# Softmax attention and an MLP on one core: units 3 to 5 take the 128-key form, with k and v loaded by SyncE

## The chip, the cores and the metric

The kernel runs on one core of a Trainium2 chip. The metric is the device time of one execution in microseconds; it is given as the median of several runs. One of the executions was recorded by the hardware profiler; its page and trace are what is read here. The core's engines are named PE (TensorE, with PEld for its weight loads), DVE (VectorE), ACT (ScalarE), POOL (GpSimd) and SP (SyncE, which here only issues DMAs).

## What is computed

q, k and v are fp32 arrays of 8 batches, 12 heads, 448 positions and 64 dimensions. Attention is computed for each head; the heads of a batch are laid side by side, which gives x with 3584 rows and 768 columns; an MLP with 2048 hidden columns follows.

```python
scores = scale * np.matmul(q, k.transpose(0, 1, 3, 2))      # scale = 1 / sqrt(64)
attn = softmax(scores)
attn_out = np.matmul(attn, v)
x = attn_out.transpose(0, 2, 1, 3).reshape(3584, 768)
h = x @ w_in                                                # 768 x 2048
g = np.maximum(0.01 * h, h)
return g @ w_out                                            # 2048 x 768
```

## The kernel before

Matrix products run on PE in bf16. Attention is tiled in units: unit u is one batch and one pair of heads (u = 6 x batch + pair, `HP` = 6 units a batch, 48 in all). Two heads of 64 dimensions fill PE's 128 rows.

A unit passes through these steps, each a function:

- Load: `load_soft` (L163) issues DMAs on POOL, which convert fp32 to bf16 on the way; `load_one` (L173) issues on SP and leaves fp32. In the first 26 us the buffers for loads are pieces of tensors that are needed only later (`rooms`: pieces of `w_in_mix` first, then of `w_mix`, `o`, `deep_mix`, `c`), each taken once.
- `cast` (L190 to L203) copies the loaded q and k into `qkb` (L190), and v into `v_old` (L198, printed as x_mix in the trace since it lies in that tensor) or `v_sb` (L201 to L203). Units 0 and 1 and the q and k of unit 2, and v of unit 0, are cast by DVE (and ACT for half of unit 0), all others by POOL. The loop `supply(u)` writes out which casts and which DMA issues POOL does in step u, in order.
- `transposes` (L301): eight PE transposes into one PSUM bank, and one copy by DVE to `qkT` (L305).
- `scores(u, c)`: one chunk c of keys against all 448 queries, for both heads; `expo(u, c)`: ACT's exp of that chunk.
- `pv(u, j)`: the exps times v with a column of ones, which gives numerator and denominator; DVE's reciprocal (L374) and multiply (L375) give x.
- `x_transposes` (L389, L390): x turned for the MLP.

There are two forms of chunking. The old form, for units below `HY` = 18, takes the 448 keys in four chunks of `SC` = 112: four pairs of matmuls (L319), four exps over 112 rows and 896 columns (L331 three times, L334 once), and pv by `pairs` (L362), 32 matmuls of 65 columns. The new form, for units from 18 on, takes three chunks of 128 keys (`KC` = 3), and the last 64 keys of both heads share one fourth chunk: one matmul over 128 rows (L322), an exp of 448 columns in place of 896 (L336), and pv by `weighted` (L343, L350): for each of four query chunks one matmul of 130 columns and six of 65. For it k and v lie in another order in the buffers (128 rows: keys 0 to 255 on rows 0 to 63, keys 256 to 447 on rows 64 to 127), so that a cast is a memset (L193), a large copy (L194) and two small ones (L195, L196) for k, and a large copy (L201) and two small ones (L202, L203) for v.

The order of the instructions on every engine is written by hand. It begins with three loads on SP (k of 0, q of 0, k of 1), nine loads of q, k and v on POOL and the first piece of w_in. Then `first(u)` runs for u = 0 to 5: scores and exps of unit u, pv of unit u - 1, the transposes of unit u + 1, x transposes of unit u - 2, and `supply(u)` for POOL. From about 25 us the first batch's MLP products (`part`, L424) are mixed with the attention of later units; from there on the order is the same for both kernels.

w_in comes in three pieces (L215) by POOL's queue, of 4, 6 and 6 blocks of 128 columns, later w_out in four. All POOL loads go through one software queue and land in the order of their issue.

## Time and profile before

| | |
|---|---|
| runs | 377.79, 378.84, 379.81 us, median 378.84 |
| profiled execution | 378.34 us, its span 376.6 us |
| granted PE clock | 0.999 |
| PE busy | 369.7 us, 98% of the span |
| DVE busy | 256.9 us, 68% |
| ACT busy | 259.6 us, 69% |
| POOL busy | 191.8 us, 51% |
| scores of units 1 to 6 start (L319) | 9.49, 12.57, 15.96, 19.09, 22.23, 25.91 us |
| pv of units 1, 2, 3, 4 starts (L362) | 13.58, 16.71, 19.85, 22.98 us |
| w_in's third piece lands | 36.8 us |

How it is read: busy shares are averages over the whole span. The page also cuts the span into 40 slices (of 9.4 us here), with a digit for each engine's busy tenths, the granted PE clock and the DMA engines. The chain of waits goes back from the last instruction to what released each step. A timeline lists groups of instructions of one engine by start; in square brackets stands the idle time before a group and what ended it. "x3" is three instructions in a group. For DMAs the rows give the count, the KB of each, and the median time from issue to landing. POOL's and SP's rows for a DMA are the issue alone.

### The profile page before, as it was taken

To read this page: it belongs to the slowest core of one execution; us is meant where nothing else is said; L and a number is where in the kernel's file an instruction comes from. 1 tells how busy PE (TensorE), PEld (TensorE's weight loads), DVE (VectorE), ACT (ScalarE), POOL (GpSimd) and SP (SyncE) were. 2 spreads that over 40 slices of the span, in tenths; PEclk is the share of its full clock that TensorE was granted. 3 is DMA by queue.
4 is the path that set the end of the run, shared out by engine and by line. 5 is a ranking of instruction groups with operands and counts; after the bars stand their busy time and mean duration, and the time that the engine had idled before them with its cause. 6 is when DMAs were issued, how large, how long until landed. Compare 5 with 4: busy or idle time off the path is not lost.

```text
span 376.6 us, 10120 instructions
## 1 busy us (share of the span) xinstructions
PE 369.7 (98%) x4008; PEld 265.7 (71%) x4008; DVE 256.9 (68%) x558; ACT 259.6 (69%) x399; POOL 191.8 (51%) x376
## 2 busy tenths in 40 slices
PE   7999999999999999999999999999999999999996
PEld 3664658756698556996569966599665995679765
DVE  4765858778666867766676665775847775685763
ACT  5997885866768776758766587666787668636721
POOL 7985871986268989624588235792347020000000
PEclk9999999999999999999999999999999999999999
DMA  9999999999499885973869648798455740321123
GB/s 155 200 203 207 191 204 201 156 159 164 93 178 143 114 163 87 197 158 60 157 121 148 144 64 86 170 147 167 61 66 98 143 110 0 79 58 45 42 65 105
DMA packets 99600, 48.08 MB, mean 128 GB/s; under 512 B 64608, under 2 KB 96352, under 8 KB 99552
## 3 DMA queue, kind: packets, MB, share of 16 engines
q0 software_dynamic: 39600, 22.47, 44.6%
q1 hardware_dynamic: 59504, 24.50, 32.6%
q8 instruction: 31, 0.51, 0.6%
q10 hardware_dynamic: 448, 0.47, 0.4%
q14 instruction: 17, 0.14, 0.1%
HBM read 45.61 MB, written 11.01 MB: 150 GB/s over the span
## 4 chain that ended last, share of the span: by engine, by line
PE 94%; DMA 2%; DVE 1%; issue 1%; POOL 1%; ACT 1%; POOLq 0%; ACTq 0%; DVEq 0%
PE g L682 30%; PE g L548 14%; PE sc L548 14%; PE sc L322 7%; PE sc L350 6%; PE g L424 4%; PE sc L319 4%; PE sc L645 4%; PE sc L362 3%; PE g L817 2%; PE sc L343 2%; DMA w_in_mix<-in_v_dram 2%; PE g L362 1%; PE g L301 1%; PE sc L424 1%
## 5 line engine op out<-in xcount | busy, mean ns | idle before, releaser
L331 ACT ACTIVATE e<-sc 128x896 bf16<-128x896 f32 (+1 forms) x144 | 123.6, 923 | 30.7 <-PE sc L322 20.8
L682 PE MATMUL g<-w_out_sb,h 128*128 128x384 bf16 (+1 forms) x440 | 84.1, 325 | 0.0
L682 PEld LDWEIGHTS <-h 128*128 128x128 bf16 x592 | 54.4, 98 | 41.4 <-issue 11.2
L537 ACT ACTIVATE h<-c 128x512 bf16<-128x512 f32 (+1 forms) x72 | 43.1, 610 | 30.2 <-DVE c L563 12.4
L548 PEld LDWEIGHTS <-w_in_sb 128*128 128x128 bf16 x576 | 54.6, 98 | 5.7
L190 POOL COPY qkb<-fq 112x512 bf16<-112x512 bf16 x34 | 23.9, 703 | 41.6 <-DMA qkT<-qkb 32.5
L548 PEld LDWEIGHTS <-w_in_mix 128*128 128x128 bf16 x432 | 40.5, 98 | 3.7
L201 POOL COPY v<-fv 128x384 bf16<-128x384 bf16 x30 | 18.5, 617 | 43.1 <-PE sc L350 40.7
L687 DVE COPY o<-g 128x384 f32<-128x384 f32 x47 | 26.0, 553 | 13.7 <-PE g L682 13.5
L350 PE MATMUL sc<-v,e 128*128 128x65 bf16 x720 | 33.3, 193 | 0.0
L322 PE MATMUL sc<-qkT 64*128 64x448 bf16 (+1 forms) x210 | 32.8, 352 | 0.0
L350 PEld LDWEIGHTS <-e 128*128 128x128 bf16 x720 | 31.1, 98 | 1.3
L974 DVE RECIPROCAL rec<-sc 112x8 f32<-112x8 f32 x42 | 8.7, 207 | 33.6 <-PE sc L350 19.1
L975 DVE TENSOR_TENSOR x<-sc,rec 112x512 bf16<-112x512 f32 x42 | 29.0, 691 | 1.6 <-DVE rec L974 0.2
L548 PE MATMUL g<-xT,w_in_sb 128*128 128x256 bf16 (+1 forms) x216 | 28.5, 268 | 0.0
L548 PE MATMUL sc<-xT,w_in_sb 128*128 128x256 bf16 (+1 forms) x216 | 28.5, 268 | 0.0
L693 DVE TENSOR_TENSOR o<-o,g 128x384 f32<-128x384 f32 x39 | 21.4, 549 | 9.1 <-PE g L682 4.4
L343 PE MATMUL sc<-v,e 128*128 128x130 bf16 x120 | 26.5, 221 | 0.0
L649 DVE TENSOR_TENSOR o<-o,sc 128x192 f32<-128x192 f32 x39 | 13.7, 351 | 17.9 <-PE sc L645 17.9
L682 PE MATMUL g<-w_mix,h 128*128 128x384 bf16 x128 | 24.6, 326 | 0.2 <-DVE o L687 0.2
L163 POOL DMA_DIRECT2D fv<-in_v_dram x32 | 20.1, 641 | 7.7 <-DMA fq<-in_q_dram 3.1
L682 PE MATMUL g<-w_mix,hmix 128*128 128x384 bf16 x112 | 21.7, 326 | 0.0
(149 smaller groups left out, 744.1 us busy)
## 6 DMA issues: line engine op xcount, KB each, us to landing
fq<-in_q_dram POOLq DMA_DIRECT2D x17, 224.0 KB, 5.7
w_out_sb<-in_moe_w_out_dram POOLq DMA_DIRECT2D x4, 768.0 KB, 13.2
out_dram<-o SPq DMA_DIRECT2D x7, 336.0 KB, 3.4
w_in_sb<-in_moe_w_in_dram POOLq DMA_DIRECT2D x2, 1152.0 KB, 12.7
out_dram<-o SPq DMA_DIRECT2D x7, 288.0 KB, 3.4
fk<-in_k_dram POOLq DMA_DIRECT2D x15, 128.0 KB, 5.9
fv<-in_v_dram POOLq DMA_DIRECT2D x15, 128.0 KB, 4.8
out_dram<-o SPq DMA_DIRECT2D x7, 240.0 KB, 3.1
```

Of the source, the lines that this page charges most:

```text
L163: nc.gpsimd.dma_start(out=t[p, :n, :, :so].rearrange("p u h so d -> p (u h) (so d)"), in_=(q, k, v)[x][b, hs, keys].rearrange("h (p so) d ...
L190: by(t[:SC, x].rearrange("p so h d -> p h so d"), f)
L322: nc.tensor.matmul(ps[:, j, :S].rearrange("p (so s) -> p so s", so=NSC), t[p, 1, c], t[p, 0, :, :SC], start=True, stop=True,)
L331: nc.scalar.activation(e[:, :, c, :], ps[:n, :, :S], AX.Exp, scale=scale)
L343: nc.tensor.matmul(ps, e[:, EM + qc * SC:EM + qc * SC + P], vt[:, 2 * KC:].rearrange("p j d -> p (j d)"), start=True, stop=False, skip_gro ...
L350: nc.tensor.matmul(ps[:, j * (D + 1):(j + 1) * (D + 1)], e[:, at:at + P], vt[:, j * KC + c], start=False, stop=(c == KC - 1), skip_group_c ...
L537: nc.scalar.activation(hs[:, m:m + 2, cols], x.rearrange("p (m t) -> p m t", m=2), AX.Prelu, alpha=0.01)
L548: nc.tensor.matmul(ps[:, j * nh:(j + 1) * nh], w[:, kk, ts(j, P)], x[:, kk], start=(first and j == 0 and kk == 0), stop=(kk == KH - 1), sk ...
L682: nc.tensor.matmul(ps[:, cols], x[:, m], w[:, m], start=(first and m == 0), stop=(m == MH - 1), skip_group_check=True,)
L687: by(o[:, at], ps[:, :NW])
L693: nc.vector.tensor_add(o[:, at], o[:, at], ps[:, :NW])
L975: nc.vector.tensor_mul(x, ps[:, :, :, :D], rec.to_broadcast([SC, 2, 2 * NP, D]))
```

## The change

Units 3, 4 and 5 take the new form. `old(u)` says which units keep the old one: 0 to 2 and 6 to 17. The functions that tested `u < HY` now test `old(u)`, and `pv` calls `weighted` for new units.

k and v of units 3 to 5 are no longer loaded by POOL. A new function `load_into` loads one of them by two SP DMAs, of 64 rows with 2 x 256 and 2 x 192 elements, in fp32, into a buffer whose first content has been cast already: k of 3 into that of q of 1; once v of unit 0 is cast, k of 4, v of 3 and v of 4 into those of v of 0, k of 1 and k of 2; in `supply(0)` k of 5 into that of q of 2 and 3 and v of 5 into that of v of 1 and 2. POOL's casts of them read fp32.

POOL's loads before the first casts are q of 1; q of 2 and 3; k of 2; v of 0; v of 1 and 2; q of 4 and 5; q and k of 6 and 7; then w_in's first piece. The table in `supply` has another order. w_in's pieces have 5, 5 and 6 blocks. Since fewer rooms are needed, three pieces of `w_mix` are no longer among them.

```diff
--- before.py
+++ after.py
@@ -127,14 +127,20 @@
     w_in_v = moe_w_in.rearrange("(ko ki) n -> ki ko n", ki=P)
     w_out_v = moe_w_out.rearrange("(ko ki) n -> ki ko n", ki=P)
 
-    raw = {}
+    FIRST = 3
+
+    def old(u):
+
+        return u < FIRST or HP <= u < HY
+
+    raw, homes = {}, {}
 
 
 
     rooms = []
     for t in (w_in_mix, w_mix):
         t = t.rearrange("p x k n -> p (x k n)")
-        for j in range(9):
+        for j in range(9) if not rooms else range(3, 9):
             rooms.append(t[:, ts(j, 4 * NSC * D)])
     for _ in range(3):
         rooms.append(o_pool.tile([P, DM], F32, name="o").bitcast(BF16)[:, :4 * NSC * D])
@@ -148,18 +154,21 @@
         n = P if x and new else SC
         if not rooms:
             return ld_pool.tile([n, 2, NSC, D], F32, name="f" + "qkv"[x])
-        return rooms.pop(0)[:n].bitcast(F32).rearrange("p (h so d) -> p h so d", h=2, so=NSC)
+        homes["last"] = rooms.pop(0).bitcast(F32).rearrange("p (h so d) -> p h so d", h=2, so=NSC)
+        return homes["last"][:n]
+
+    split = ((slice(0, D), NSC, slice(0, NSC * D)), (slice(D, P), KC, slice(NSC * D, S)))
 
     def load_soft(u, n, which):
         b, hp = divmod(u, HP)
         hs = slice(2 * hp, 2 * hp + 2 * n)
         for x in which:
             new = x > 0 and u >= HY
-            t = room(x, new).rearrange("p h so d -> p (h so d)").bitcast(BF16)
+            t = room(x, new)
+            homes[u, x] = homes["last"]
+            t = t.rearrange("p h so d -> p (h so d)").bitcast(BF16)
             t = t.rearrange("p (u h so d) -> p u h so d", u=2, h=2, so=NSC)
-            for p, so, keys in ((slice(0, D), NSC, slice(0, NSC * D)), (slice(D, P), KC, slice(NSC * D, S))) if new else (
-                (slice(0, SC), NSC, slice(0, S)),
-            ):
+            for p, so, keys in split if new else ((slice(0, SC), NSC, slice(0, S)),):
                 nc.gpsimd.dma_start(
                     out=t[p, :n, :, :so].rearrange("p u h so d -> p (u h) (so d)"),
                     in_=(q, k, v)[x][b, hs, keys].rearrange("h (p so) d -> p h (so d)", so=so),
@@ -170,10 +179,20 @@
     def load_one(u, x, queue):
         b, hp = divmod(u, HP)
         t = room(x, False)
+        homes[u, x] = homes["last"]
         queue.dma_start(
             out=t.rearrange("p h so d -> p h (so d)"),
             in_=(q, k, v)[x][b, 2 * hp:2 * hp + 2].rearrange("h (p so) d -> p h (so d)", so=NSC),
         )
+        raw.setdefault(u, {})[x] = t
+
+    def load_into(u, x, t):
+        b, hp = divmod(u, HP)
+        for p, so, keys in split:
+            nc.sync.dma_start(
+                out=t[p, :, :so].rearrange("p h so d -> p h (so d)"),
+                in_=(q, k, v)[x][b, 2 * hp:2 * hp + 2, keys].rearrange("h (p so) d -> p h (so d)", so=so),
+            )
         raw.setdefault(u, {})[x] = t
 
     def load(u, parts=(0, 1, 2)):
@@ -186,7 +205,7 @@
         for x in parts:
             f = raw[u].pop(x)
             t = qkb[u % NB]
-            if x < 2 and (x == 0 or u < HY):
+            if x < 2 and (x == 0 or old(u)):
                 by(t[:SC, x].rearrange("p so h d -> p h so d"), f)
             elif x == 1:
                 if u < HY + NB:
@@ -194,7 +213,7 @@
                 by(t[:, 1, :KC].rearrange("p so h d -> p h so d"), f[:, :, :KC])
                 by(t[:D, 1, KC, 0], f[:D, 0, KC])
                 by(t[D:, 1, KC, 1], f[:D, 1, KC])
-            elif u < HY:
+            elif old(u):
                 by(v_old[:, u % NV, :, :, :D], f)
             else:
                 t = v_sb[u % NV]
@@ -203,7 +222,7 @@
                 by(t[D:, 2 * KC + 1, :D], f[:D, 1, KC])
 
     w_steps = []
-    for lo, hi in ((0, 4), (4, 10), (10, MD)):
+    for lo, hi in ((0, 5), (5, 10), (10, MD)):
         w_steps.append([t[:, :, lo * P:hi * P] for t in (w_in_sb, w_in_v)])
     for i in range(4):
         w_steps.append([t[:, ts(i // 2 + 2 * (i % 2), MD // 4)] for t in (w_out_sb, w_out_v)])
@@ -220,12 +239,12 @@
     ident = const_pool.tile([P, P], BF16)
     make_identity(nc, ident)
     load_soft(1, 1, (0,))
-    load_soft(2, 2, (0, 1))
+    load_soft(2, 2, (0,))
+    load_soft(2, 1, (1,))
     load_soft(0, 1, (2,))
     load_soft(1, 2, (2,))
-    load_soft(4, 2, (0, 1))
-    load_soft(3, 2, (2,))
-    load_soft(5, 1, (2,))
+    load_soft(4, 2, (0,))
+    load_soft(6, 2, (0, 1))
     load_w(1)
 
     warm = h_mix.rearrange("p m c t -> p (m c t)")[:, :512]
@@ -292,7 +311,7 @@
         return bank.bitcast(BF16)
 
     def transposes(u, bank=None):
-        n = SC if u < HY else P
+        n = SC if old(u) else P
         t, flat = qkb[u % NB], qkT[u % NQ].rearrange("p i c s -> p (i c s)")[:, :2 * NSC * n]
         for parts in ((1,), (0,)) if u == 0 else ((0, 1),):
             tr = turn_tile(bank)[:, :2 * NSC * n].rearrange("p (i s) -> p i s", i=2)
@@ -312,7 +331,7 @@
         ps = next_slot()
         t = qkT[u % NQ]
         sc_t[u, c] = ps
-        if u < HY:
+        if old(u):
             t = t.rearrange("p i c s -> p (i c s)")
             for j in range(2):
                 p = slice(j * D, (j + 1) * D)
@@ -325,11 +344,11 @@
 
     def expo(u, c):
         e, ps = e_sb[u % NE], sc_t.pop((u, c))
-        n = SC if u < HY else P
+        n = SC if old(u) else P
         if c < KC:
             e = e[:n, :EM].rearrange("p (j c s) -> p j c s", j=2, c=KC)
             nc.scalar.activation(e[:, :, c, :], ps[:n, :, :S], AX.Exp, scale=scale)
-        elif u < HY:
+        elif old(u):
             e = e_old[u % NE][:n, :2 * S].rearrange("p (j s) -> p j s", j=2)
             nc.scalar.activation(e, ps[:n, :, :S], AX.Exp, scale=scale)
         else:
@@ -367,14 +386,19 @@
 
         bank = next_bank() if bank is None else bank
         ps = bank[:, :NSC * (D + 1)].rearrange("p (q d) -> p q d", q=NSC)
-        pairs(u, j, ps)
         if j == 0:
             x_t[u] = x_pool.tile([SC, NSC, 2, D], BF16, name="x")
+        if old(u):
+            pairs(u, j, ps)
+            x = x_t[u][:, :, j, :]
+        else:
+            n = 2 * (D + 1)
+            for y in range(NP):
+                weighted(u, j * NP + y, bank[:, y * n:(y + 1) * n])
+            x = x_t[u][:, j * NP:(j + 1) * NP].rearrange("p q j d -> p (q j) d")
         rec = r_pool.tile([SC, NSC, 1], F32, name="rec")
         nc.vector.reciprocal(rec, ps[:SC, :, D:])
-        nc.vector.tensor_mul(
-            x_t[u][:, :, j, :], ps[:SC, :, :D], rec.to_broadcast([SC, NSC, D])
-        )
+        nc.vector.tensor_mul(x, ps[:SC, :, :D], rec.to_broadcast([SC, NSC, D]))
 
     def x_transposes(u, bank=None):
         b, hp = divmod(u, HP)
@@ -850,13 +874,15 @@
 
     def supply(u):
 
-        for what, n, *parts in {0: [('load', 6, (0, 1)), ('qk', 3), ('v', 1), ('v', 2), ('load', 6, (2,))], 1: [('qk', 4), ('v', 3), ('load', 8, (0, 1))], 2: [('qk', 5), ('v', 4), ('w', 1)], 3: [('qk', 6), ('v', 5), ('w', 1)], 4: [('qk', 7), ('v', 6), ('load', 10, (0, 1)), ('load', 8, (2,))], 5: [('qk', 8), ('v', 7), ('load', 10, (2,)), ('load', 12)]}[u]:
+        for what, n, *parts in {0: [('qk', 3), ('v', 1), ('v', 2), ('into', 5, 1, (2, 0)), ('into', 5, 2, (1, 2))], 1: [('qk', 4), ('load', 6, (2,)), ('v', 3)], 2: [('qk', 5), ('load', 8, (0, 1)), ('qk', 6), ('v', 4), ('w', 1)], 3: [('v', 5), ('w', 1)], 4: [('qk', 7), ('v', 6), ('load', 10, (0, 1)), ('load', 8, (2,))], 5: [('qk', 8), ('v', 7), ('load', 10, (2,)), ('load', 12)]}[u]:
             if what == "qk":
                 cast(n, (0, 1))
             elif what == "v":
                 cast(n, (2,))
             elif what == "load":
                 load(n, *parts)
+            elif what == "into":
+                load_into(n, parts[0], homes[parts[1]])
             else:
                 load_w(n)
 
@@ -884,6 +910,9 @@
         if u == 0:
             cast(2, (0, 1), fast)
             cast(0, (2,), fast)
+            load_into(4, 1, homes[0, 2])
+            load_into(3, 2, homes[1, 1])
+            load_into(4, 2, homes[2, 1])
         if u + 1 < HP:
             supply(u)
         if u < 2:
@@ -898,6 +927,7 @@
 
     transposes(0)
     cast(1, (0, 1), fast)
+    load_into(3, 1, homes[1, 0])
     for u in range(HP):
         first(u)
```

## The prediction

> **What bounds the kernel now.** I read the busy shares first, then the slices, the chain of waits, the timelines of ACT and POOL, and the DMA rows. All durations come from one execution: 378.34 us, of which 376.6 are the span and 1.74 lie around it. The runs' median, 378.84, is 0.50 above it.
>
> ```profile
> PE 369.7 (98%) x4008; PEld 265.7 (71%) x4008; DVE 256.9 (68%) x558; ACT 259.6 (69%) x399; POOL 191.8 (51%) x376
> ACT  5997885866768776758766587666787668636721
> POOL 7985871986268989624588235792347020000000
> DMA  9999999999499885973869648798455740321123
> ```
>
> PE is idle for only 6.9 us of the span. The change ends with unit 5, about 26 us in (three slices), so that is where to look. By windows PE is busy 9.19 us of 10 to 20, 9.79 of 20 to 30 and all of 30 to 40. The part after the first 10 us has 1.02 us of PE idling to win. ACT is busy all of 10 to 20, POOL 9.81 us of it, and the DMA digit is full for the first ten slices: four resources are near their limits together. The chain shows which ends last:
>
> ```profile
> 3.71 6.83 DMA w_in_mix<-in_v_dram
> 10.57 0.44 DVE x_mix L198
> 11.05 0.67 PE g L362 x16
> ...
> 15.96 0.55 PE sc L319 x4
> 16.51 0.36 PE g L389 x4
> 16.88 0.51 PE g L362 x16
> 17.39 0.48 PE sc L319 x4
> 17.87 0.51 PE g L301 x8
> 18.39 0.02 issue
> 18.41 0.64 DVE qkT L305
> 19.05 0.05 issue
> ```
>
> The landing of unit 0's v starts the steady part. Then each unit is a loop: scores, x transposes, pv, scores, eight transposes, DVE's copy qkT, and the next scores, 15.96 to 19.09 = 3.13 us. ACT has almost the same pitch:
>
> ```profile
> 16.43 2.53 ACT L331 ACTIVATE e<-sc 112x896 bf16<-112x896 f32 x3
> 18.83 0.93 ACT L334 ACTIVATE c<-sc 112x896 bf16<-112x896 f32 x1
> 19.63 2.55 ACT L331 ACTIVATE e<-sc 112x896 bf16<-112x896 f32 x3
> ```
>
> 16.43 to 19.63 is 3.20 us for four exps, 0.80 start to start. The two bounds are 0.07 apart.
>
> **Exps, scores, transposes, pv.** In each of units 3, 4 and 5 three long exps and one 128x448 (the form that L336 has later, 543 ns against some 920) replace four long ones: 0.37 us less ACT work a unit, 1.1 in all. It buys little, because the 3.13 loop remains and grows. Eight 112-column transposes take 0.41 us from first start to last start (17.80 to 18.21). At 128 columns that is 0.41 x 128/112, +0.058. L305 takes 624 ns for 896 columns and 392 for 448, 0.52 ns a column, so 1024 columns are +0.066. Scores: a 128-row matmul of 448 columns takes 0.19, as a 64-row pair does, so nothing. pv: two groups of seven take 0.50 (later, 0.25 a group), against 0.51 for L362's 16. The loop becomes 3.13 + 0.058 + 0.066 - 0.01 = 3.24, and ACT's 2.83 a unit lies beneath it. Three units: **+0.35**. Against ACT's 3.20, which the chain goes through once (the scores at 22.23), it would be +0.12, and if the wider copies hid entirely, three units would gain 3 x 0.07 = 0.2; I take the chain's 3.13.
>
> **Unit 0's v.** Its load stands behind k of units 2 and 3 in the soft queue, and will stand behind k of 2 alone: 112 KB less, 0.58 by the queue's spacing (1.17 for 224 KB). But k of 3 now comes on SP, in two DMAs issued once DVE has cast q of 1 (about 8.05), at 0.45 each. So it shares the engines in the same stretch, in fp32. Bounds: -0.58 (no sharing) to +1.0 (k fully ahead, as slowly as SP's k of 1). Packets that share cost about what they spare, so I take **+0.2**.
>
> **POOL.** This is the danger.
>
> ```profile
> 11.59 1.17 POOL L190 COPY qkb<-w_in_mix 112x512 bf16<-112x512 bf16 x2
> 12.70 1.17 POOL L198 COPY x_mix<-w_in_mix 112x512 bf16<-112x512 bf16 x2
> 27.83 1.17 POOL L190 COPY qkb<-w_mix 112x512 bf16<-112x512 bf16 x2
> ```
>
> Removed: three DMA issues net before unit 5's work (0.70 each), and the front's stalls at 7.98, 9.06 and 10.19 (0.78, 0.41, 0.28) shrink, so casts could start near 9 instead of 11.59. Added: a k cast of the new form is memset 0.147, large copy 0.445, two small ones 0.29 each = 1.17 against 0.556; a v cast 0.45 + 0.58 = 1.03 against 0.556. Three units: 3 x (0.61 + 0.47) = 3.3 us. No row shows a POOL copy from fp32. Bounds: no dearer (its slope, 612 - 501 ns over 128 elements, is 0.87 ns an element, above even the 0.42 us / 512 = 0.82 that DVE takes from fp32) to 0.42/0.29 = 1.45 times the bf16 one, which is DVE's ratio, or 6 x 0.2 = 1.2 us more. I take the low end, since the POOL slope is the nearest row.
>
> [...]
>
> What POOL waits for is now the landing on SP's queue:
>
> ```profile
> w_in_mix<-in_k_dram SPq DMA_DIRECT2D x1, 224.0 KB, 2.9
> w_in_mix<-in_q_dram SPq DMA_DIRECT2D x1, 224.0 KB, 3.3
> w_in_mix<-in_k_dram SPq DMA_DIRECT2D x2, 224.0 KB, 4.4
> ```
>
> The first row is k of 0 alone (0 to 1 us), the last k of 0 and 1 (0 to 30), so k of 1, which flies while the soft queue fills, takes 2 x 4.4 - 2.9 = 5.9. For k of 3, last half issued at 8.5, I take 3.3, since its halves are smaller: 11.8, with 11.4 and 14.4 as bounds. Then POOL has k3 at 12.8 (its q earlier), v1 at 13.4 where PE wanted it at 13.58, v2 13.95, q4 and k4 15.65, v3 17.4 behind a DMA issue, q5 and k5 19.4 (k5 lands near 14.6 + 3.3 = 17.9: SP first issues six DMAs of k4, v3, v4 behind v0's copy at 11.0), then two DMAs 20.8, q6 and k6 22.0, v4 23.0 (PE wants 22.98 plus the 0.55 of PE's delay), w 23.9, v5 24.9, w 25.7, q7 and k7 26.8, v6 27.4, three DMAs 29.5, q8 and k8 30.6. PE's transposes of unit 8 start at 30.36 + 0.55 = 30.9. Cost **0**, with a cover of some 0.3 at v4 and unit 8; each us beyond that costs a us of PE, and POOL then makes it good only in the 4.23 it waits before 38.04. SP has nothing else to do until it transposes for later units, so its waits delay only its own loads.
>
> **The soft queue.** It is a FIFO, full from about 8 to 63 us. Six half-loads leave it and the same six come as fp32 elsewhere, in pieces twice as many: 0.58 to 0.85 us each of engine time (0.85 by k of 1's 5.9 against q of 0's 3.3, spread over the packets between), so everything behind comes 0 to 1.6 later; I take 0.8. The first w piece grows by 192 KB (+0.94) and goes behind q and k of 6 and 7 (+2.34), but ahead of it 2.92 leave (k of 4 and 5, v of 3 to 5): it lands near 19.63 + 0.4 + 0.8 = 20.8, and PE's first L424 on the chain starts at 25.22. The second piece shrinks by as much as the first grows, so nothing changes behind it. The third piece of w lands at 36.76 and DVE waits for it (L473). After it DVE idles 0.39 before its next row, and PE comes 0.55 later itself: 0.94 of cover against 0.8. Cost **0**, up to 0.7 at the bound.
>
> The Trainium skill (DMA: Bandwidth & Descriptors, sections "Issuing engines are not separate DMA queues" and "Rules for kernel authors") says that all queues end on the same 16 engines and that transfers to disjoint partition halves serialize. The full DMA digits agree, and by it the six loads would gain nothing from leaving the soft queue.
>
> **Sum.** 0.35 + 0.2 + 0 + 0 = +0.55: the profiled execution would be 378.9, and **379.4** stands against the median. About 0.5% (1.9 us) is what a measurement of this kernel can tell from no change.
>
> **Rivals.** *POOL falls behind (slower):* k3 lands late behind the full soft queue. The place is POOL's cast of k3, with v1 queued behind it; the point is a landing later than 12.15, from which pv of unit 1 waits. At k of 1's 5.9, k3 is there at 14.4, cast at 15.5, v1 at 16.0: 2.4 past 13.58, less the 0.35 that waits anyway: +2.0 on the sum, 381.4. For it: that row, and the DMA digits; k5 at 20.4 would do +1.3 in the same way. Against: smaller halves, a start later than the first rush. *The head gets shorter (faster):* v0 is 0.58 earlier, POOL's earlier start and ACT's 1.1 us remove the 0.2-us stalls before each unit's scores, of which L319 has 1.3 us between 10 and 40. I price it at -1.1: 377.7. For it: ACT never idles from 6.72 to 26.2, and the scores of 22.23 wait for ACT. Against: the other units' scores wait for DVE's qkT, which gets longer. *The transfers reach the path:* 1.6 us later w pieces, 0.7 past the cover, and w_out's second piece, at 55.13 for PE's 55.77, a few tenths: about 380.2. *It doesn't do what it says:* the built program has the three short exps, the three wider qkT copies and twelve more SP DMAs, so I give it nothing.
>
> **Chances.** Forecast 0.42, POOL behind 0.38, shorter head 0.13, transfers 0.07. Forecast and transfers stay within 0.5%. Half of the shorter-head cases come out over 1.9 us faster or near it: faster 0.07, the rest same. POOL behind splits around 1.9 us; with its spread to 383 I leave 0.35 slower, same 0.58. The range, 377.5 to 382.2, takes in the shorter head and most of POOL's; the forecast's own is 378.6 to 380.6.
>
> **What would show it.** Three exps of 128x448 near 0.54 with ACT idle before scores; qkT copies of 0.69; scores 3.24 apart for units 4 to 6; POOL's k3 cast done before 13; PE at L362 of unit 1 waiting for no POOL copy; w's third piece near 37.6. An L362 or weighted matmul that waits for a POOL copy, or POOL idle "<-DMA" from k_dram above 1 us, makes the forecast wrong upward; scores less than 3.13 apart make it wrong downward.

## The result

The changed kernel takes 383.69 us (median of 6 runs, 382.93 to 384.86), the kernel before 378.3 us (6 runs, 377.79 to 379.81). The ratio is 1.0139, with a 95% interval of 1.0115 to 1.0164: 5.4 us slower. The forecast of 379.4 us, counted from 378.84 (the median of the first three of those six), and its range missed it. The measured time lies on the side of the rival in which POOL falls behind, but 2.3 us beyond that rival's 381.4. Three later executions with a lower granted clock (one of e7_four, one of the kernel before, and the profiled one of e15_best_order, of which no landings are given) are left out of the medians.

The profiled execution took 383.39 us, its span is 381.6, 5.0 more than before. First the lines of the changed kernel's page that answer to those shown ahead of the prediction, with the slices of the granted PE clock:

```profile
PE 371.1 (97%) x3993; PEld 267.1 (70%) x3993; DVE 257.1 (67%) x558; ACT 259.5 (68%) x399; POOL 192.2 (50%) x388
ACT  6676886767668787576875777847778559627721
POOL 8479593698157978834568445594438020000000
PEclk9789999999999999999999999999999999999999
DMA  9989999999599895993668938789335830221123
```

Busy sums hardly moved; the slices did. POOL falls from 9 to 4 tenths in the second slice, ACT is no longer full, and the clock drops in slices 2 and 3. A table by stage shows it closer (start and end, length, then busy time of PE, PEld, DVE, ACT and POOL, granted clock, DMA share, GB/s); the first table is the changed kernel, the second the kernel before:

```profile
10.00:16.00 6.00, 2.85 (x52) 2.08 (x51) 2.14 (x6) 4.47 (x6) 1.56 (x5) 0.90 1.29 226
16.00:20.00 4.00, 3.98 (x46) 2.89 (x47) 1.48 (x4) 1.73 (x2) 2.80 (x7) 0.50 1.17 237
20.00:24.00 4.00, 3.73 (x55) 2.54 (x51) 2.42 (x7) 3.08 (x4) 2.23 (x7) 0.79 0.98 209
24.00:31.00 7.00, 6.59 (x100) 4.34 (x96) 4.56 (x13) 5.94 (x8) 6.69 (x15) 1.00 0.76 93
```

```profile
16.00:20.00 4.00, 3.79 (x65) 2.44 (x66) 2.56 (x7) 4.00 (x6) 4.00 (x7) 1.00 1.32 198
24.00:31.00 7.00, 7.00 (x101) 4.58 (x100) 4.04 (x12) 5.30 (x8) 7.00 (x13) 1.00 1.18 212
```

PE is busy 2.85 us of the first six; from 16 to 20 it is busy throughout, but at half the clock (46 matmuls, against 65 before in the same stretch); and from 24 to 31 the DMA engines move 93 GB/s (212 before). Those are three different troubles. The starts of the scores of units 1 to 6 date the loss: 8.76, 11.93, 19.69, 23.73, 26.97 and 30.78 us against 9.49, 12.57, 15.96, 19.09, 22.23 and 25.91. The changed kernel is 0.7 ahead at units 1 and 2, 3.7 behind at unit 3 and 4.9 behind at unit 6. After that little changes: the first product with w_out starts 5.6 later (77.54 against 71.96), and the end is 5.0 later.

The first trouble, in PE's and POOL's timelines of the changed kernel (start, length, engine, instruction; in brackets the idle time before it and what ended it):

```profile
12.74 0.37 PE L413 MATMUL g<-ident,x 112*128 112x112 bf16 x4 [0.25 <-DVE x L401]
16.02 0.32 PE L381 MATMUL g<-x_mix,e 112*128 112x65 bf16 x3 [2.91 <-POOL x_mix L217]
```

```profile
14.32 0.50 POOL L213 CAST qkb<-w_in_mix 128x384 bf16<-128x384 f32 x1 [5.51 <-DMA w_in_mix<-in_k_dram]
15.35 1.17 POOL L217 COPY x_mix<-w_in_mix 112x512 bf16<-112x512 bf16 x2
...
23.44 0.50 POOL L213 CAST qkb<-w_in_mix 128x384 bf16<-128x384 f32 x1 [1.56 <-DMA w_in_mix<-in_k_dram]
...
27.84 0.84 POOL L234 DMA_DIRECT2D w_in_sb<-in_moe_w_in_dram  x1
...
29.65 0.83 POOL L234 DMA_DIRECT2D w_in_sb<-in_moe_w_in_dram  x1
```

POOL waits 5.51 us for k of 3; v of 1 is queued behind it, and PE waits 2.91 us for that. Later POOL waits 1.56 for k of 5. POOL also issues w_in's second and third pieces, at 27.84 and 29.65 (19.23 and 23.25 before): that stands behind the same waits. The soft queue has nothing to do meanwhile, which is the 93 GB/s, and the third piece lands at 42.55 instead of 36.76.

Why k of 3 is late shows in the rows for its two DMAs (KB, and us to landing), and in the packets of the two queues from 8 to 11.5 us, both of the changed kernel:

```profile
w_in_mix<-in_k_dram SPq DMA_DIRECT2D x1, 128.0 KB, 6.2
w_in_mix<-in_k_dram SPq DMA_DIRECT2D x1, 96.0 KB, 6.1
```

```profile
q0 software_dynamic: 1360, 0.67, 143.1%
q1 hardware_dynamic: 1, 0.00, 0.1%
```

SP issued them at 7.31 and 8.10. For 3.5 us after that one packet moved on SP's queue and 1360 on POOL's. The landings are 13.55 and 14.19. SP's packets begin to move at about the time at which the soft load of q of 4 and 5 (issued at 5.06) lands, 11.40; from then on the queues share. But q and k of 6 and 7, which POOL had also issued before (at 5.76 and 6.45), landed only at 13.3 and 15.2, so SP didn't wait for all that stood ahead of it, and why it began just then isn't shown.

The chain of waits of the changed kernel goes through the second wait, from the issue of k of 5 to pv of unit 4:

```profile
14.26 9.06 DMA w_in_mix<-in_k_dram
...
23.44 0.50 POOL qkb L213
...
26.96 0.46 POOL v L220
...
27.66 0.24 POOL v L222
27.91 0.04 issue
27.95 0.22 PE g L362
```

So three limits arrive at nearly the same time: PE's own progress after the first wait, POOL's cast of v of 4, and w_in's later pieces. The experiments take them one by one.

### The profile page after: what moved, and what is told of

It reads as the page before. It is cut to its first block, busy times and chain, and to the rows that moved or that the text cites. A ratio compares the mean times of both kernels' runs of the same rounds, so it can differ in the third digit from the quotient of the medians.

```text
span 381.6 us, 10123 instructions
## 1 busy us (share of the span) xinstructions
PE 371.1 (97%) x3993; PEld 267.1 (70%) x3993; DVE 257.1 (67%) x558; ACT 259.5 (68%) x399; POOL 192.2 (50%) x388
## 4 chain that ended last, share of the span: by engine, by line
PE 91%; DMA 5%; POOL 1%; issue 1%; DVE 0%; ACT 0%; SPq 0%; POOLq 0%; ACTq 0%
PE g L706 30%; PE g L572 14%; PE sc L572 14%; PE sc L341 7%; PE sc L369 6%; PE g L448 4%; DMA w_in_mix<-in_k_dram 4%; PE sc L669 4%; PE sc L381 3%; PE sc L338 3%; PE g L841 2%; PE sc L362 2%; DMA w_in_mix<-in_q_dram 1%; PE g L320 1%; PE sc L448 1%
## 5 line engine op out<-in xcount | busy, mean ns | idle before, releaser
L209 POOL COPY qkb<-fq 112x512 bf16<-112x512 bf16 x34 | 22.7, 667 | 45.5 <-DMA qkT<-qkb 36.4
L220 POOL COPY v<-fv 128x384 bf16<-128x384 bf16 x30 | 17.9, 596 | 40.7 <-PE sc L369 38.0
L341 PE MATMUL sc<-qkT 64*128 64x448 bf16 (+1 forms) x231 | 36.8, 356 | 0.6 <-DVE qkT L324 0.6
L369 PEld LDWEIGHTS <-e 128*128 128x128 bf16 x792 | 34.3, 98 | 1.5 <-issue 0.2
```

The lines of the kernel that those rows point to most:

```text
L209: by(t[:SC, x].rearrange("p so h d -> p h so d"), f)
L341: nc.tensor.matmul(ps[:, j, :S].rearrange("p (so s) -> p so s", so=NSC), t[p, 1, c], t[p, 0, :, :SC], start=True, stop=True,)
L369: nc.tensor.matmul(ps[:, j * (D + 1):(j + 1) * (D + 1)], e[:, at:at + P], vt[:, j * KC + c], start=False, stop=(c == KC - 1), skip_group_c ...
```

## The experiments

All ratios are to the kernel before, run on the same chip. In diffs, lines are those of the changed kernel unless it says otherwise; of `supply`'s table they show only the entries that differ.

| run | ratio, 95% interval | median us | w_in's pieces 2, 3 land | first MLP product starts |
|---|---|---|---|---|
| before | 1 | 378.3 | 31.07, 36.76 | 25.06 |
| changed kernel | 1.0139 (1.0115 to 1.0164) | 383.69 | 36.83, 42.55 | 29.93 |
| e1_k3_early | 1.0161 (1.0144 to 1.0178) | 384.17 | 36.98, 42.65 | 29.79 |
| e2_w_late | 1.0150 (1.0135 to 1.0165) | 383.58 | 37.06, 42.74 | 30.22 |
| e3_both | 1.0173 (1.0154 to 1.0193) | 384.47 | 36.78, 42.38 | 29.75 |
| e4_warm | 1.0182 (1.0165 to 1.0199) | 384.96 | 37.02, 42.55 | 29.96 |
| e5_sp_old_form | 1.0148 (1.0125 to 1.0172) | 383.67 | 36.30, 42.03 | 29.30 |
| e6_order | 1.0115 (1.0096 to 1.0134) | 382.12 | 35.48, 41.07 | 27.30 |
| e7_four | 1.0138 (1.0122 to 1.0153) | 383.05 | 36.35, 41.97 | 29.39 |
| e8_order_old_form | 1.0091 (1.0074 to 1.0108) | 381.66 | 34.27, 39.98 | 26.23 |
| e10_soft_later | 1.0178 (1.0159 to 1.0198) | 384.64 | 38.93, 44.51 | 30.74 |
| e11_before_w_late | 1.0141 (1.0128 to 1.0155) | 383.60 | 36.00, 41.59 | 25.05 |
| e12_before_more_sp | 1.0119 (1.0104 to 1.0135) | 382.78 | 35.91, 41.49 | 28.83 |
| e13_before_v_first | 1.0001 (0.9992 to 1.0009) | 377.97 | 31.28, 36.86 | 24.85 |
| e14_w_in_time | 1.0156 (1.0123 to 1.0189) | 383.67 | 33.04, 38.71 | 30.16 |
| e14_again | 1.0144 (1.0116 to 1.0172) | 382.78 | 32.11, 37.71 | 29.96 |
| e15_best_order | 1.0132 (1.0114 to 1.0151) | 383.09 | | |
| e16_w_in_time_warm | 1.0143 (1.0122 to 1.0164) | 383.49 | 33.18, 38.78 | 30.18 |

**The form or the loads.** In e5_sp_old_form units 3 to 5 keep the old form.

```diff
-    FIRST = 3
+    FIRST = HP
...
-        for p, so, keys in split:
-            nc.sync.dma_start(
-                out=t[p, :, :so].rearrange("p h so d -> p h (so d)"),
...
+        t = t[:SC]
+        nc.sync.dma_start(
+            out=t.rearrange("p h so d -> p h (so d)"),
```

> Units 3 to 5 keep the old form (four chunks of 112), but their k and v come by SP in fp32 as in the changed kernel, each as one DMA. POOL's casts are 3.3 us shorter, PE and ACT do what they did before. Theory A (the loads' landing is the cause, not the form): k of 3 lands after 13, pv of unit 1 waits for 2.5 to 3 us again, and the time is 382.5 to 384. Theory D (the new form's dearer casts are the cause): at most 379.5.

The loss is the same. k of 3 as one DMA issued at 7.30 lands at 13.57; PE's wait for v of 1 is 1.77 us, shorter than the 2.5 to 3 expected. So neither the 128-key chunks nor POOL's dearer casts are needed for the loss. What is left of the change here, the SP loads together with the new order of POOL's issues and the pieces of 5, 5 and 6 blocks, is enough.

**One edit at a time.** e1_k3_early loads k of 3 at once into a part of `w_mix` that nothing has used; e2_w_late moves w_in's first piece behind the cast of v of 3; e3_both does both.

```diff
+    spare = [w_mix.rearrange("p x k n -> p (x k n)")[:, ts(j, 4 * NSC * D)].bitcast(F32).rearrange(
+        "p (h so d) -> p h so d", h=2, so=NSC) for j in range(3)]
...
     load_one(1, 1, nc.sync)
+    load_into(3, 1, spare[0])
...
-    load_into(3, 1, homes[1, 0])
```

```diff
     load_soft(6, 2, (0, 1))
-    load_w(1)
...
-1: [('qk', 4), ('load', 6, (2,)), ('v', 3)],
+1: [('qk', 4), ('load', 6, (2,)), ('v', 3), ('w', 1)],
```

> k of unit 3 is loaded by SP at once into a buffer that nothing has used, so it waits neither for DVE's cast nor behind the soft queue. Theory A (two waits in series: POOL's wait for k of 3, then its wait for k of 5, behind which v of 4 is cast; the second ends last): PE's 2.91 us wait for v of 1 goes, but k of 5 still lands near 22 instead of 23.3, so v of 4 is cast near 26.9 instead of 27.9: 382.7 us, about 1 less. Theory B (the wait for k of 3, with the lower clock behind it, is all): back to 378 to 379.

> w_in's first piece is issued by POOL behind the cast of v of 3 instead of in front of all casts; nothing else moves. Theory A: SP's loads no longer share the engines with it from 15 us on, k of 5 lands before 20.5 instead of 23.3 and POOL's wait for it goes; but the first wait of 2.9 us and the lower clock stay and pace PE instead, so only 0.3 to 0.7 us come back: 383.0 to 383.4. Theory B: no change, 383.7. Theory C (the wait for k of 5 is all): 379 to 380.

> Both single edits together: k of 3 by SP at once into an unused buffer, and w_in's first piece issued behind the cast of v of 3. Theory A (waits in series, each edit alone only bares the next): what stays is k of 4, whose SP load is issued about 10.7 behind q of 4 and 5 and q and k of 6 and 7 in the soft queue and lands near 16 to 16.5; k of 5 lands before 19. PE waits about 0.5 for unit 4's k and at 30 us for w_in's first piece: 380 to 382. Theory B: each wait by itself, the gains of the two single runs (none and none) add up to none: 383.7.

None came out faster than the changed kernel. In e1 PE no longer waits for v of 1, but SP's next load, k of 4, issued at 10.72 and 11.35, lands at 17.64 and 18.81, PE waits 1.5 us for it, k of 5 still lands at 23.14, and pv of unit 4 starts only at 27.81, released by POOL's cast of v of 4 (27.95 in the changed kernel). w_in's pieces come as late as before. In e2 k of 5 lands at 18.22 instead of 23.32, as expected, but the wait for k of 3 stays, and PE then waits 1.06 us for w_in's first piece. In e3 PE runs units 1 to 5 without a stall, and then waits 1.32 for v of 4 and 3.18 for w_in's first piece; the third lands at 42.38. I had expected 380 to 382 from e3. Removing a wait only bared the next, as theory A says, but its times were wrong. In e1 it had k of 5 near 22 and no wait for k of 4. In e3 its sum didn't fit its own wait: a first MLP product near 30 us is already 4.7 later than the kernel before (29.75 measured), and w_in's later pieces were left out besides.

e3 gives the form's price free of such waits. Its scores of units 3, 4 and 5:

```profile
15.75 0.55 PE L343 MATMUL sc<-qkT 64*128 64x448 bf16 x4 [0.27 <-DVE qkT L326]
...
19.00 0.55 PE L343 MATMUL sc<-qkT 64*128 64x448 bf16 x4 [0.27 <-DVE qkT L326]
...
22.25 0.55 PE L343 MATMUL sc<-qkT 64*128 64x448 bf16 x4 [0.28 <-DVE qkT L326]
```

They are 3.25 apart; the working had 3.24. In e8_order_old_form below, the old form under the same SP loads, they are 3.13 apart (15.31, 18.44, 21.58), and ACT's four long exps keep pace.

**SP's loads and the soft queue.** e10_soft_later keeps k of 3 as in the change, but cuts what POOL issues ahead of it, so that the soft queue ends with v of 1 and 2 there.

```diff
-    load_soft(4, 2, (0,))
-    load_soft(6, 2, (0, 1))
-    load_w(1)
...
-{0: [('qk', 3), ('v', 1), ('v', 2), ('into', 5, 1, (2, 0)), ('into', 5, 2, (1, 2))], 1: [('qk', 4), ('load', 6, (2,)), ('v', 3)],
+{0: [('qk', 3), ('load', 4, (0,)), ('v', 1), ('v', 2), ('into', 5, 1, (2, 0)), ('into', 5, 2, (1, 2)), ('load', 6, (0, 1))], 1: [('qk', 4), ('v', 3), ('w', 1), ('load', 6, (2,))],
```

> k of 3 stays on SP in q of 1's used buffer, issued at about 7.3 as in the changed kernel, but in front of POOL's casts only the soft loads up to v of 1 and 2 are issued; q of 4 and 5 comes behind k of 3's cast, q and k of 6 and 7 behind unit 5's loads, w_in's first piece behind v of 3. Theory A (SP's load moves once the soft loads issued before it are through): v of 1 and 2 lands near 10.3 as before, k of 3 by 11.5 to 12.2 instead of 14.2, so that PE waits at most 0.7 for v of 1; total 378 to 380.5. Theory F (an SP load takes 6 us whatever is ahead): k of 3 at 13.5 or later, total above 381.5.

The chain of that run has the load of k of 3:

```profile
8.68 3.10 DMA w_in_mix<-in_k_dram
```

3.1 us instead of 6.1, landed at 11.78, as theory A expected. Theory F falls: an SP load isn't slow in itself, it is held up by the soft queue's backlog. From 7.9 to 9 us POOL's queue moves 436 packets and SP's none; from 9 to 10.5, as POOL's run out, it is 192 and 222. (The last soft load, v of 1 and 2, is reported landed only at 11.34.) That SP must wait for every soft load issued before, as theory A puts it, isn't shown; in the changed kernel two of them landed after SP's packets had begun to move. PE's wait for v of 1 shrank to 0.88. But the total was 384.64, not 378 to 380.5: the DMA engines were half idle from 10 to 15 us (124 GB/s), and all that was postponed came later, w_in's third piece at 44.51.

e6_order and e8_order_old_form load k of 3 early and issue q and k of 6 and 7 and w_in's first piece behind SP's second group; e8 has the old form besides.

```diff
-    load_soft(6, 2, (0, 1))
-    load_w(1)
...
-('into', 5, 2, (1, 2))], 1: [('qk', 4), ('load', 6, (2,)), ('v', 3)],
+('into', 5, 2, (1, 2)), ('load', 6, (0, 1))], 1: [('qk', 4), ('v', 3), ('w', 1), ('load', 6, (2,))],
```

> k of 3 by SP at once into an unused buffer; q and k of 6 and 7 are issued behind unit 5's loads instead of in front of all casts, w_in's first piece behind the cast of v of 3, then v of 6 and 7: the soft queue in front of SP's second group ends with q of 4 and 5. Theory A (SP's loads are late because of the soft loads issued ahead of and beside them): k of 4 lands before 14.5, k of 5 before 18.5, no PE wait for POOL above 0.3 us before 25 us: 377.5 to 379.5, within 0.5% of the kernel before. Theory E (two DMAs of 64 rows each in fp32 are too dear on the engines wherever they stand): k of 5 after 20, 381 to 383.

> The same order as e6_order, but units 3 to 5 keep the old form, with k and v by SP in fp32 as one DMA each. The difference to e6_order is the form alone: the prediction's working gives the new form +0.35 us, so this run is 0.2 to 0.6 faster than e6_order if POOL is in time in both; if POOL's dearer casts matter (3.3 us of them), it is 1 to 3 us faster; if ACT's 1.1 us matters, it is slower by up to 1.

These are the best of the SP versions, and still 0.9% to 1.2% slower. e6 has k of 5 at 19.94 and, up to the first MLP product, two stalls of PE left, 1.46 us for v of 4 and 0.59 for w_in's first piece. e8 shows the trade plainly, in PE's timeline:

```profile
21.58 0.55 PE L339 MATMUL sc<-qkT 64*128 64x448 bf16 x4 [0.21 <-ACT e L351]
...
26.23 0.93 PE L449 MATMUL sc<-xT,w_in_sb 128*128 128x448 bf16 x4 [1.63 <-DMA w_in_sb<-in_moe_w_in_dram]
```

At unit 5 it is 0.65 ahead of the kernel before (22.23). Then PE stands for w_in's first piece, landed at 26.18 instead of 19.63, and the third piece is 3.2 late. Behind that wait the granted clock is 0.50 from 28 to 31 us; what that costs here wasn't tried. The 0.46 us between e6 and e8 are within their intervals, so they don't settle the form's price; the starts above do.

e15_best_order was a third order of POOL's issues.

```diff
-    load_soft(6, 2, (0, 1))
-    load_w(1)
...
+{0: [('qk', 3), ('load', 6, (0, 1)), ('v', 1), ('v', 2), ('into', 5, 1, (2, 0)), ('into', 5, 2, (1, 2)), ('w', 1)], 1: [('qk', 4), ('v', 3), ('load', 6, (2,)), ('load', 8, (0, 1))], 2: [('qk', 5), ('v', 4), ('qk', 6), ('w', 1)],
```

> The change with k of 3 by SP at once into an unused buffer and with POOL's issues moved so that the soft queue never runs dry and no cast waits for them: q and k of 6 and 7 behind the cast of k of 3, w_in's first piece behind v of 2, v of 6 and q, k of 8 behind v of 3, v of 4 ahead of q and k of 6. If the loss is one of order, it is within 0.3 of the kernel before. If SP's loads cost 0.79 us each (the third piece 4.7 later for six of them in e12_before_more_sp) against 0.58 on the soft queue, 1.3 us stay and the form adds up to 0.35: w's third piece at 38 to 38.7, 379 to 380.

At 383.09 it won nothing over the changed kernel, and both of its expectations were wrong. So no order that was tried comes within 0.9% of the kernel before; that none exists isn't shown.

**The price of an SP load.** e12_before_more_sp adds six such loads, which nothing reads, to the kernel before (lines of that kernel):

```diff
     cast(0, (2,), fast)
+    load_into(4, 1, homes[0, 2])
+    load_into(3, 2, homes[1, 1])
+    load_into(4, 2, homes[0, 1])
...
-('v', 1), ('v', 2), ('load', 6, (2,))
+('v', 1), ('v', 2), ('into', 5, 1, (0, 0)), ('into', 5, 2, (1, 2)), ('load', 6, (2,))
...
     cast(1, (0, 1), fast)
+    load_into(3, 1, homes[1, 0])
```

> The kernel before, with six more loads on SP as the changed kernel issues them (two pieces each, 224 KB of fp32, into used buffers), which nothing reads: the price of such a load for the soft queue, which keeps all its own loads. Theory G (the engines' time goes by bytes written, 200 to 240 GB/s): each costs 0.93 to 1.15 us, w_in's third piece lands 5.6 to 6.9 later, 42.4 to 43.7, total 383 to 385. Theory H (by rows of 512 or 1024 bytes alike, as a soft load of one unit): 0.58 each, 3.5 later, 40.2, total 380.5 to 382.

w_in's second piece lands 4.84 later and the third 4.73: about 0.8 us for each load, between the two theories, against 0.58 for the same unit's load on the soft queue. By that, the six moved loads should cost the DMA engines some 6 x 0.22 = 1.3 us, an estimate. The run also shows how full the queue is: 4.7 us more of transfers cost 4.5 us of time (1.19% of 378), first as PE's waits for q and k of 6, behind which the granted clock is 0.50 up to 33.5 us:

```profile
10.19 16.58 DMA w_mix<-in_k_dram
...
26.91 0.62 POOL qkb L203
...
27.59 0.56 PE g L314 x4
```

**w_in's pieces alone.** e11_before_w_late has nothing of the change; in the kernel before, POOL only issues w_in's second and third pieces later, with q and k of 10 and v of 8 behind them, as the changed kernel does.

```diff
-2: [('qk', 5), ('v', 4), ('w', 1)], 3: [('qk', 6), ('v', 5), ('w', 1)], 4: [('qk', 7), ('v', 6), ('load', 10, (0, 1)), ('load', 8, (2,))], 5: [('qk', 8), ('v', 7),
+2: [('qk', 5), ('v', 4)], 3: [('qk', 6), ('v', 5)], 4: [('qk', 7), ('v', 6)], 5: [('qk', 8), ('w', 2), ('load', 10, (0, 1)), ('load', 8, (2,)), ('v', 7),
```

> The kernel before, with nothing of the change, but POOL issues w_in's second and third pieces behind the cast of q and k of 8 (about 27.8 us, as the changed kernel does) instead of behind v of 4 and v of 5, and q, k of 10 and v of 8 behind them. Theory W (POOL's late issue of w_in's pieces sets the end in the changed kernel, whatever else was late): the third piece lands at 42 to 43 instead of 36.8, and the time is 382.5 to 384, the whole loss. Theory P (PE's own waits up to unit 6 are the loss): units 0 to 6 are as before, PE waits somewhat for w_in, at most 380.

1.0141, the whole loss, from late pieces with the loads behind them. Units 0 to 6 run as before (first product at 25.05), while the DMA engines move only 59 GB/s from 25 to 30. Then PE waits 1.99 us for the second piece, and DVE 4.53 us for it and 3.19 for the third, which the chain names. From 36.4 to 39.7 us the granted clock is 0.50, so what each piece costs alone isn't shown. PE's row, the chain and the windows of that run:

```profile
36.05 2.18 PE L424 MATMUL g<-xT,w_in_sb 128*128 128x448 bf16 x6 [1.99 <-DMA w_in_sb<-in_moe_w_in_dram]
```


```profile
27.00 14.58 DMA w_in_sb<-in_moe_w_in_dram
41.61 0.57 DVE w_in_mix L473
```

```profile
25.00:30.00 5.00, 5.00 (x72) 3.01 (x69) 2.78 (x9) 3.78 (x5) 4.70 (x8) 1.00 0.47 59
30.00:40.00 10.00, 8.01 (x46) 3.05 (x44) 3.45 (x5) 6.29 (x11) 5.18 (x7) 0.83 1.12 197
```

Late pieces are thus enough by themselves. Are they all? e14_w_in_time is the changed kernel with POOL's issues of v of 6, q and k of 8 and both pieces moved ahead of the wait for k of 5.

```diff
-('into', 5, 2, (1, 2))], 1: [('qk', 4), ('load', 6, (2,)), ('v', 3)], 2: [('qk', 5), ('load', 8, (0, 1)), ('qk', 6), ('v', 4), ('w', 1)], 3: [('v', 5), ('w', 1)],
+('into', 5, 2, (1, 2)), ('load', 6, (2,)), ('load', 8, (0, 1)), ('w', 2)], 1: [('qk', 4), ('v', 3)], 2: [('qk', 5), ('qk', 6), ('v', 4)], 3: [('v', 5)],
```

> The changed kernel, but POOL issues v of 6, q and k of 8 and w_in's second and third pieces behind the cast of v of 2 (16 to 20 us) instead of behind the casts of q and k of 5, v of 4 and v of 5. The waits for k of 3 and k of 5 stay; the third piece lands near 38.5 instead of 42.55. Theory W (only the late pieces set the end): 379.5 to 380. Theory V (PE's own waits are nearly as long): v of 4 is cast near 26.6 and pv of unit 4 starts 3.6 later than in the kernel before, so 381 to 382. No change at all, 383.7, would speak against both.

The third piece lands at 38.71, DVE no longer waits for it, and nothing is won: 1.0156, in the repetition 1.0144. Theory W falls, and theory V's 381 to 382 was too low; by the expectation's own words, no change speaks against both. What is left is PE's own lateness: it waits 3.85 us for v of 1 and then runs at half the clock.

```profile
17.04 0.32 PE L381 MATMUL g<-x_mix,e 112*128 112x65 bf16 x3 [3.85 <-POOL x_mix L217]
```

Its first product starts at 30.16, 5.1 late, and that is already the whole loss. The late pieces and PE's own lateness are two losses of about the same size side by side.

**The lower clock.** e4_warm (the changed kernel) and e16_w_in_time_warm (e14) keep PE at work during the wait for v of 1, with 50 and 66 idle matmuls.

```diff
         if old(u):
+        if (u, j) == (1, 0):
+            for _ in range(66):
+                nc.tensor.matmul(bank[:, :P], warm[:, :P], warm[:, :P], start=True, stop=True)
             pairs(u, j, ps)
```

> PE does 50 idle matmuls of 128 columns (2.7 us) while it waits for v of 1, so that it isn't idle there; nothing else changes, and the result of them is overwritten. Theory A: the granted clock stays at 1.00 from 10 to 25 us (0.74 and 0.92 in two windows of the changed kernel), PE reaches pv of unit 4 some 2 us earlier and waits there for v of 4 behind k of 5: 383.7, within 0.4. Theory B: the lower clock's 2 us come back: 381.5 to 382.

> e14_w_in_time with 66 idle matmuls of 128 columns (3.5 us) on PE while it waits for v of 1. If the lower clock behind the wait is part of the loss, it goes: granted clock 1.00 from 10 to 30 us, pv of unit 4 about 1.5 to 2 us earlier, and 381 to 382, that is 1.5 to 2 faster than e14_w_in_time. If the wait is all, or if v of 4 is cast only at 27.8 anyway, less than 0.5 comes back.

> e14_w_in_time once more, beside e16_w_in_time_warm on the same chip: 382.7 to 384.5 as before.

The clock obeys. Windows of e14_w_in_time and of e16_w_in_time_warm for 15 to 20 us:

```profile
15.00:20.00 5.00, 2.96 (x34) 2.14 (x34) 0.67 (x3) 1.40 (x2) 4.54 (x9) 0.50 1.16 238
```

```profile
15.00:20.00 5.00, 4.66 (x87) 3.90 (x85) 1.51 (x5) 1.68 (x2) 4.26 (x9) 1.00 1.16 234
```

0.50 becomes 1.00, and the time doesn't improve in either. e4, at 384.96, even lies above theory A's 383.7 and its 0.4. Its trace shows what PE then runs into, v of 4, at nearly the time at which pv of unit 4 starts in the changed kernel (27.95):

```profile
27.98 0.22 PE L362 MATMUL g<-v,e 128*128 128x130 bf16 x1 [1.27 <-POOL v L222]
```

In e16 POOL, held up by the late k of 3 and five issues, has the q and k of unit 4 cast only when PE wants them at 22.2 (two short waits, 0.36 and 0.19); scores of unit 4 start at 24.25, against 24.04 in e14_again. So the lower clock fills time that PE would have waited anyway. It is no separate part of the loss in these two kernels; the expectation of 381 to 382 was wrong.

**Two parts of the change.** e7_four is the changed kernel with w_in's pieces of 4, 6 and 6 blocks (`((0, 4), (4, 10), (10, MD))`).

> The changed kernel with w_in's pieces of 4, 6 and 6 blocks as before. The first piece is 192 KB shorter, so SP's loads beside it land up to 0.9 earlier, k of 5 near 22.5 instead of 23.3; the second piece is as much longer, so the third lands 0.5 to 0.9 earlier only by what POOL issues earlier. Theory W: 0.5 to 0.9 faster than the changed kernel, 382.8 to 383.2. Rival: the five blocks are what costs, 379 to 380.

1.0138, not to be told from the changed kernel's 1.0139; the third piece lands 0.6 earlier. e13_before_v_first tries whether unit 0's v can be had earlier in the kernel before, without SP.

```diff
-    load_soft(2, 2, (0, 1))
+    load_soft(2, 2, (0,))
+    load_soft(2, 1, (1,))
     load_soft(0, 1, (2,))
     load_soft(1, 2, (2,))
+    nc.gpsimd.dma_start(
+        out=homes[2, 1][:SC, 1].rearrange("p h so d -> p h (so d)"),
+        in_=k[0, 6:8].rearrange("h (p so) d -> p h (so d)", so=NSC),
+    )
...
-('qk', 3), ('v', 1), ('v', 2)
+('v', 1), ('qk', 3), ('v', 2)
```

> The kernel before, all loads on the soft queue, but k of 3 is a load of its own behind v of 1 and 2 instead of with k of 2, and POOL casts v of 1 ahead of q and k of 3. Unit 0's v lands 0.58 earlier with no other load made later that PE waits for. Theory W: PE is 0.5 earlier up to unit 6, but w_in's third piece lands when it did, 36.8, with 0.39 of idling behind it: at most 0.4 us faster, 377.5 to 378.0 beside the kernel before. Rival: PE's 0.58 is kept to the end, 377.3; POOL's further issue makes it late, 379 or more.

v of 0 lands at 9.03 instead of 10.54. Of these 1.5 us, 1.0 is not the edit's: q of 1, loaded ahead of it and as before, lands at 6.7 instead of 7.7 in this execution. PE's first MLP product starts 0.2 earlier, and the time is the same: 1.0001, 0.9992 to 1.0009. The third piece lands at 36.86 and DVE waits 3.3 us for it (2.6 before), which fits theory W: what PE gains in the head, w_in's third piece takes back.

## Why the prediction was wrong

The step that failed is POOL's term, "Cost **0**, with a cover of some 0.3 at v4 and unit 8". It stands on two landings of SP's loads, and both were taken too early.

- "For k of 3, last half issued at 8.5, I take 3.3": it took 6.1 and landed at 14.19 instead of 11.8, inside the bounds given but at their other end. POOL waited 5.51 us for it and PE 2.91.
- "k5 lands near 14.6 + 3.3 = 17.9": it landed at 23.32, behind SP's own seven DMAs that shared with the soft queue. So v of 4, which PE would want at 22.98 + 0.55, was cast only at 27.9.

Each is enough to hold PE up. With k of 3 early and k of 5 still at 23.14 (e1) nothing is won, and with k of 5 at 18.22 and k of 3 still late (e2, where PE also waits for w_in's first piece) nothing either. So a right figure for k of 3 alone wouldn't have given the right time for the right reason.

The row chosen for k of 3, q of 0, had flown before the soft queue filled. The row not chosen, k of 1's 5.9, comes out near 6.1, but that is partly luck: from 4.5 to 7.5 us k of 1's queue moved 113 packets beside POOL's 823, while k of 3's moved one in 3.5 us and then shared. The rival named the place, the point (12.15) and the wait (2.4; 2.91 measured, v of 1 at 16.0 as it said). It was given 0.38 and was the better forecast.

The second error is in the size, and would have missed even from that rival. "each us beyond that costs a us of PE, and POOL then makes it good only in the 4.23 it waits" followed POOL's casts, but not the DMAs that POOL issues behind them. The working had the third piece of w_in at 36.76 + 0.8, hidden by 0.94 of cover. It came 5.8 later, since its issue moved from 23.25 to 29.65. e11 shows that late pieces, with the loads behind them, cost 5.3 us by themselves; e14 shows that bringing them in time gives nothing back as long as PE is late too.

The other terms:

- The wider loop, +0.35: right, 3.25 us a unit measured against 3.24. That ACT's 1.1 us buy nothing is right too, as the scores wait for DVE's qkT.
- Unit 0's v, +0.2: wrong in sign. It landed at 8.98 instead of 10.54. Of that, 0.6 is the change's: v comes 2.2 us behind q of 1 instead of 2.8, which is the bound without sharing, since k of 3 moved no packets there. The other 1.0 is q of 1 itself, at 6.7 instead of 7.7, though no load ahead of it was changed (e10_soft_later, with the same loads up to there, has 7.6). So most of the 0.7 us lead at units 1 and 2 is scatter between executions.
- SP's loads at 0.58 to 0.85 on the engines, 0.8 in all: about 0.8 each by e12, against 0.58 on the soft queue, so 1.3 in all, within the bounds.
- SP "has nothing else to do" and so delays only its own loads: true of SP, but those loads were enough. k of 5's second half, issued at 14.26, took 9.06 us, with seven others of SP's ahead of it and w_in's first piece beside them. The rival's bound of 20.4 was also too low.
- POOL's copies from fp32 at no more than bf16 ones: 0.50, 0.23 and 0.23 us measured, the durations of the kernel before's bf16 rows (501, 230 and 232 ns). The low end that was taken is right.
- The rule from the Trainium skill, DMA: Bandwidth & Descriptors, "Issuing engines are not separate DMA queues", held in that the six loads gained nothing by leaving the soft queue (0.8 us each on the engines against 0.58). But the section also says that DMAs of several issuers interleave, and here the trace differs: k of 3 moved one packet in 3.5 us beside 1360 of the soft queue, and interleaved only afterwards.

What stays open: how large each of the three limits would be with the other two gone, since no run brought the time back; e11 alone shows one of them by itself. Nor was the new form run with k and v left on the soft queue, or the new order of POOL's issues with the old loads, so the share of the order isn't separated from that of the loads.

## What to carry to other kernels

When a transfer moves to another queue, price its landing by a row that flew against the same backlog, not by the fastest row of that queue, and do so for each load of the series, not for the first alone. Where an engine both computes and issues transfers, follow a late operand through to the transfers queued behind it in that engine's program: their landing can cost as much as the stall itself. And when several resources run full together, removing one wait shows the next one, so look for runs that make one limit late alone in the good kernel, rather than only for runs that take one away in the bad one.

## What the runs showed that I had not expected

- A DMA issued on SP while POOL's queue had a backlog moved almost nothing at first: 1 packet against 1360 from 8 to 11.5 us, landing after 6.1 us; it landed after 3.1 with a shorter backlog (e10_soft_later). Once both ran, they shared, 569 and 572 packets from 14 to 19 us, and together moved 237 GB/s from 16 to 20 us, against 198 of the soft queue alone in the kernel before.
- Short waits of PE were enough to lower the granted clock. After the 2.91 us in the changed kernel it was 0.50 until 21.6 us, and after 1.51 us in e1_k3_early it was 0.50 from 19.5 to 26.3; after 1.46 us in e6_order it stayed at 1.00 (23 to 30 us). With idle matmuls in the gap it stayed at 1.00 (e16_w_in_time_warm). No run here shows what decides between them.
